# Bucketed attention and a gated product: the first chunk's probabilities in float32, turned by TensorE

## Chip, cores and metric

The kernel runs on one core of one Trainium2 chip. The metric is the device time of one execution in microseconds (us); the number given is the median of three runs. One execution was profiled as well.

The engines are TensorE (PE in the profile; its weight loads are PEld), VectorE (DVE), ScalarE (ACT), GpSimd (POOL) and SyncE (SP). SP issues all DMAs of this kernel, the plain ones and those that turn (transpose) a tile of 16-bit numbers on its way.

## The reference

```python
# q, k, v: (4, 8, 768, 64); proj: (64, 6); w_a, w_b: (512, 1536); w_out: (1536, 512)
q_bits = (np.einsum('bhsd,dk->bhsk', q, proj) > 0); k_bits = (np.einsum('bhsd,dk->bhsk', k, proj) > 0)
q_bucket, k_bucket = sum(bits * 2 ** arange(6))      # 64 buckets
mask = q_bucket[:, :, :, None] == k_bucket[:, :, None, :]
scores = np.where(mask, q @ k.T / sqrt(64), -1e9)
attn = np.exp(scores - max); attn = attn / (sum + 1e-9)
x = (attn @ v), heads side by side                   # (3072, 512)
out = ((x @ w_a) * (x @ w_b)) @ w_out                # (3072, 512) float32
```

Attention is computed only between queries and keys whose six sign bits agree. Its output feeds a gated product of two matrices and a third one.

## The kernel before, in words

Work is cut into 12 chunks: 4 batches of 3 chunks of 256 query rows, with all 8 heads. A chunk has 16 tiles, one for each head and block of 128 query rows (`qtile`), in two halves of 8. A tile is named by batch, chunk, half, pair of heads in the half, head in the pair and block of rows.

Numbers of float32 accuracy are kept as a high and a low float16 part, so that TensorE works on float16 throughout. For each pair of heads K is split (`kprep`): the natural layout is scaled and cut into parts, turned so that the head dimension lies on the partitions, multiplied with `proj` (`buckets`), the six signs are written as extra columns, and a second tile with the signs is turned too. That makes two turned tiles per pair, kTB and kTA. `turn` does a turn in one of two ways: by one transposing DMA (queue SP), or by twelve TensorE transposes into PSUM and a copy of PSUM by ACT or DVE. In batch 0 the first `K_BY_PE` pairs take TensorE, all others DMA. Q goes the same way (`qprep`).

A tile then runs through these steps, with their lines in the profile:
- scores, two times two products of 384 columns (PE, L1029), into a PSUM buffer of two
- the row's maximum (DVE, L1041), its width and bias (L1050, L1057 or L1063)
- the exponential, with the row sums as a by-product (ACT, L1073), into e, float32. Its bias holds ln 2^14, so that the float16 parts keep their accuracy
- a cast of e to float16 (DVE L1081, ACT L1082 or POOL L1083) and the rest e - hi (POOL L1093 or DVE L1097), into the two halves of a2
- one transposing DMA of a2 to at (L1103)
- 18 products of 64 columns, hi x V hi, hi x V lo, lo x V hi (PE, L1112), into the half's av

V is split into vh and vl for this (`vprep`: the maximum by L755 or L758, vh by L793, vl by L805). At a half's end av is divided by the sums (`su_end`), and at a chunk's end x is scaled and turned; for the first and the last chunk by eight float32 transposes on TensorE (px, L1250), for the others by DMA.

The second stage (`moe`) takes a chunk's turned x: 24 groups of 12 products (ab, L1313) with the two first matrices, a gate on ACT and DVE (L1327, L1335), a split of it (L1343, L1355), and 12 groups of 6 products with the third matrix (o, L1365). Before that the 18 blocks of weights are loaded and split as well: an ACT pass (L554), the low words (ACT L562 or POOL L568), a merge on DVE (L577), the high half (ACT L654, POOL L657 or DVE) and the low half (POOL L662 or DVE L666).

Nothing is scheduled while the kernel runs. `Plan` records each step as an operation with an engine, possibly with alternatives on other engines, and the list `ORDER` names operations in the order in which they are issued: a number n below 10000 is operation n, 10000 + n its first alternative, 20000 + n its second. A negative entry -n puts n filler products on TensorE (`fill`, tile "warm", L1469), whose results are not used. Each engine works through its own instructions strictly in this order, and so does SP's queue.

Of the kernel before, what the change touches and what calls it, by code (L numbers as in the profile page):

```python
# [21 lines left out]
P = 128  # L22
# [53 lines left out]
def constants():  # L76
# [17 lines left out]
K_BY_PE = 4  # L94
# [289 lines left out]
def attention_moe(ctx: ExitStack, tc: tile.TileContext, q, k, v, proj, w_a, w_b, w_out, cst, cst_w, out):  # L384
# [341 lines left out]


    HOME_K0 = [("wo0", 1, cp), ("wo1", 1, cp), ("raw", NRAW, p2), ("raw", NRAW, p2)]
    HOME_V0 = [("a2", NA, p2)] * 2 + [("at", NAT, p2)] * 2
    xT, kT, vv, qT, xs, tsq = {}, {}, {}, {}, {}, {}  # L730

    def load_heads(src, b, h0, n, name, key, hold=(), home=("raw", NRAW, p2)):
# [775 lines left out]
```

## Time and profile before

| what | value |
|---|---|
| median of three runs | 901.48 us (900.17 to 902.36) |
| the profiled execution's own time | 899.88 us |
| its span, first to last instruction | 898.1 us |
| PE busy | 858.3 us (96%) |
| DVE busy | 652.5 us (73%) |
| ACT busy | 548.6 us (61%) |
| POOL busy | 450.3 us (50%) |

The span is what the profile covers; some 1.8 us of the execution lie around it. Busy time is summed over the whole span and says nothing about a stage. A matmul's busy time includes the end of its pipeline, so matmuls that follow each other overlap: what one costs TensorE is read from start to start. The filler products count as busy.

### The profile page before, as it was taken

To read this page: it belongs to the slowest core of one execution; us is meant where nothing else is said; L and a number is where in the kernel's file an instruction comes from. 1 tells how busy PE (TensorE), PEld (TensorE's weight loads), DVE (VectorE), ACT (ScalarE), POOL (GpSimd) and SP (SyncE) were. 2 spreads that over 40 slices of the span, in tenths; PEclk is the share of its full clock that TensorE was granted. 3 is DMA by queue.
4 is the path that set the end of the run, shared out by engine and by line. 5 is a ranking of instruction groups with operands and counts; after the bars stand their busy time and mean duration, and the time that the engine had idled before them with its cause. 6 is when DMAs were issued, how large, how long until landed. Compare 5 with 4: busy or idle time off the path is not lost.

```text
span 898.1 us, 23606 instructions
## 1 busy us (share of the span) xinstructions
PE 858.3 (96%) x9444; PEld 652.4 (73%) x9444; DVE 652.5 (73%) x1564; ACT 548.6 (61%) x1056; POOL 450.3 (50%) x389
## 2 busy tenths in 40 slices
PE   4778899999999999999999999999999999999997
PEld 3566677777777777777777777777777777777775
DVE  6999998988887669778876766777888854752210
ACT  6999899987655656556653556645566545543222
POOL 2468957776527653552533263673543545452111
PEclk9999999999999999999999999999999999999999
DMA  8799999999998999978869689898899966754000
GB/s 311 240 270 272 178 237 236 185 205 195 204 183 169 155 170 183 194 153 176 167 125 157 102 159 176 155 206 159 151 194 165 157 116 115 118 102 72 1 25 24
DMA packets 435806, 147.37 MB, mean 164 GB/s; under 512 B 407408, under 2 KB 428016, under 8 KB 435696
## 3 DMA queue, kind: packets, MB, share of 16 engines
q1 hardware_dynamic: 435696, 145.86, 83.4%
q8 instruction: 74, 1.21, 0.6%
q14 instruction: 36, 0.29, 0.1%
HBM read 37.82 MB, written 6.29 MB: 49 GB/s over the span
## 4 chain that ended last, share of the span: by engine, by line
PE 77%; DVE 7%; ACT 3%; DMA 2%; issue 2%; POOL 0%; ACTq 0%; DVEq 0%; POOLq 0%; SPq 0%
PE ab L1313 38%; PE o L1365 19%; PE s L1029 11%; PE av L1112 9%; DMA at<-a 2%; DVE mx L1041 2%; ACT e L1073 1%; DVE xz L1215 1%; ACT a L1082 1%; DVE g L1335 0%; DVE wab L577 0%; PE b_q L819 0%; PE b_k L819 0%; DVE wmx L638 0%; DVE width L1050 0%
## 5 line engine op out<-in xcount | busy, mean ns | idle before, releaser
L1313 PE MATMUL ab<-xT,wab 128*128 128x256 f16 x3456 | 407.7, 273 | 2.2 <-DVE g L1335 2.2
L1313 PEld LDWEIGHTS <-wab 128*128 128x128 f16 x3456 | 332.3, 98 | 55.2 <-issue 2.8
L1093 POOL TENSOR_TENSOR a<-e,a 128x768 f16<-128x768 f32 x147 | 251.2, 1714 | 111.9 <-ACT a L1082 50.2
L1073 ACT ACTIVATE e<-s,bias,width 128x768 f32<-128x768 f32 x192 | 189.7, 988 | 61.1 <-DVE bias L1063 49.1
L1355 POOL TENSOR_TENSOR g<-g,g 128x256 f16<-128x256 f32 x144 | 102.1, 709 | 244.2 <-ACT g L1343 150.8
L1365 PE MATMUL o<-wo,g 128*128 128x512 f16 x864 | 208.7, 379 | 0.0
L1041 DVE TENSOR_REDUCE mx<-s 128x1 f32<-128x768 f32 x192 | 181.5, 949 | 35.2 <-PE s L1029 34.5
L1335 DVE SCALAR_TENSOR_TENSOR g<-ab,wlow,a 128x256 f32<-128x256 f32 x132 | 63.4, 481 | 139.3 <-ACT a L1327 127.0
L1327 ACT ACTIVATE a<-ab,wcut 128x256 f32<-128x256 f32 x144 | 67.7, 470 | 156.7 <-PE ab L1313 148.9
L1112 PEld LDWEIGHTS <-at 128*128 128x128 f16 x3456 | 122.3, 98 | 29.2 <-DMA at<-a 10.9
L1365 PEld LDWEIGHTS <-g 128*128 128x128 f16 x864 | 81.4, 98 | 74.7 <-issue 0.2
L1112 PE MATMUL av<-vh,at 128*128 128x64 f16 x2304 | 126.3, 193 | 9.1 <-DMA at<-a 8.6
L1029 PE MATMUL s<-kTA_k,qTA_q 128*128 128x384 f16 x384 | 93.8, 326 | 5.1 <-ACT e L1073 2.6
L1029 PE MATMUL s<-kTB_k,qTB_q 128*128 128x384 f16 x384 | 93.8, 326 | 0.0
L1082 ACT CAST a<-e 128x768 f16<-128x768 f32 x95 | 78.4, 828 | 2.8 <-DMA at<-a 1.4
L1083 POOL CAST a<-e 128x768 f16<-128x768 f32 x54 | 46.5, 860 | 53.7 <-ACT e L1073 48.2
L1112 PE MATMUL av<-vl,at 128*128 128x64 f16 x1152 | 65.1, 193 | 0.0
L1057 ACT ACTIVATE bias<-mx,width 128x1 f32<-128x1 f32 x98 | 28.4, 292 | 55.9 <-DVE width L1050 55.7
L1343 ACT CAST g<-g 128x256 f16<-128x256 f32 x97 | 38.8, 400 | 35.6 <-DVE g L1335 30.6
L1029 PEld LDWEIGHTS <-qTB_q 128*128 128x128 f16 x384 | 37.5, 98 | 24.9
L1029 PEld LDWEIGHTS <-qTA_q 128*128 128x128 f16 x384 | 34.4, 98 | 24.6 <-issue 8.3
L1097 DVE TENSOR_TENSOR a<-e,a 128x768 f16<-128x768 f32 x45 | 43.5, 967 | 3.8 <-ACT a L1082 3.4
(151 smaller groups left out, 824.3 us busy)
## 6 DMA issues: line engine op xcount, KB each, us to landing
rk_k<-in_k_dram SPq DMA_DIRECT2D x16, 384.0 KB, 4.4
rq_q<-in_q_dram SPq DMA_DIRECT2D x12, 512.0 KB, 5.0
vr<-in_v_dram SPq DMA_DIRECT2D x16, 384.0 KB, 4.2
raw_w<-in_moe_w_b_dram SPq DMA_DIRECT2D x12, 512.0 KB, 5.8
raw_w<-in_moe_w_a_dram SPq DMA_DIRECT2D x12, 512.0 KB, 6.2
raw_wo<-in_moe_w_out_dram SPq DMA_DIRECT2D x12, 512.0 KB, 6.1
out_dram<-ob SPq DMA_DIRECT2D x24, 256.0 KB, 3.1
at<-a SPq DMA_TRANSPOSE x192, 4.2
```

Of the source, the lines that this page charges most:

```text
L1029: nc.tensor.matmul(ps.t[:, jj, :HALF], lhsT=x.t[:, uq, :], rhs=y.t[:, h * NT + jj * 3 : h * NT + jj * 3 + 3, :].rearrange("p t x -> p (t x)"),
L1041: lambda: nc.vector.tensor_reduce(out=mx.t[:, u : u + 1], in_=halves(ps.t), axis=AX.XY, op=ALU.max, negate=True),
L1073: lambda: nc.scalar.activation(flat2(e.t), halves(ps.t), AF.Exp, bias=bias.t[:, u : u + 1], scale=width.t[:, u : u + 1], accum_out=sm.t[:, ...
L1082: ("ACT", 0.725, lambda: nc.scalar.copy(out=a2.t[:, 0], in_=e.t), False),
L1083: ("POOL", 0.9, lambda: nc.gpsimd.tensor_copy(out=a2.t[:, 0], in_=e.t), False),
L1093: lambda: nc.gpsimd.tensor_tensor(out=a2.t[:, 1], in0=e.t, in1=a2.t[:, 0], op=ALU.subtract),
L1112: nc.tensor.matmul(av.t[:, u, :], lhsT=at.t[:, a + kt, :], rhs=w.t[:, h, kt, :], start=i == 0, stop=i == 3 * NT - 1,)
L1313: nc.tensor.matmul(pl.t[:, m, :CH], lhsT=wt(m, wi, cc, f), rhs=xt.t[:, :, xi * NC + cc, :], start=i == 0, stop=i == 3 * NC - 1,)
L1327: lambda a=a, pl=pl, gr=gr: nc.scalar.activation(a.t, pl.t[:, 0, :CH], AF.Copy, scale=wcut[:, gr : gr + 1]),
L1335: lambda a=a, g32=g32, pl=pl, cut=cut: nc.vector.scalar_tensor_tensor(out=g32.t, in0=pl.t[:, 1, :CH], scalar=cut, in1=a.t, op0=ALU.mult, o ...
L1355: lambda g=g, g32=g32: nc.gpsimd.tensor_tensor(out=g[1].t, in0=g32.t, in1=g[0].t, op=ALU.subtract),
L1365: nc.tensor.matmul(po.t[:, u, :], lhsT=g[gi].t[:, us], rhs=wo[f // 2].t[:, f % 2, wi * DM : (wi + 1) * DM], start=f % per_q == 0 and i == ...
```

## The change

Three things are done, and the list `ORDER` is another one.

1. The first chunk of batch 0 (`F32_UNITS = ((0, 0),)`, 16 tiles) no longer splits its probabilities. e stays float32, six TensorE transposes turn it into PSUM (tile et), ACT or DVE copies it to SBUF (tile ec), and six float32 products of 64 columns multiply it with V as it was loaded (v32, tile vr). For these tiles the cast, the subtraction, the transposing DMA and the 18 float16 products are gone; the exponential's bias and the division are adapted, since nothing is scaled there.
2. `K_BY_PE` goes from 4 to 2: the pairs 2 and 3 of batch 0 are turned by DMA, two turns each, like those of all other batches.
3. V's pairs 0 to 3 of batch 0 are loaded into other buffers (`HOME_V0`): three of tag "at" and one of tag "a2".

```diff
-K_BY_PE = 4
+K_BY_PE = 2
+F32_UNITS = ((0, 0),)
...
 ORDER = [
-    1, 5, 7, 2, 4, 13, 0, 41, 53, 61, 8, 300, 301, 27, 10014, 3, 9, 297, 6, 10, 296, 11, 15, 16, 277, 17, 278, 274,
...
-    HOME_V0 = [("a2", NA, p2)] * 2 + [("at", NAT, p2)] * 2
-    xT, kT, vv, qT, xs, tsq = {}, {}, {}, {}, {}, {}
+    HOME_V0 = [("at", NAT, p2)] * 3 + [("a2", NA, p2)]
+    xT, kT, vv, v32, qT, xs, tsq = {}, {}, {}, {}, {}, {}, {}
...
         vr = load_heads(v, b, 2 * hp, 2, f"vr_{n}", key, hold=[vh, vl], home=("raw", NRAW, p2) if b else HOME_V0[hp])
+        v32[b, hp] = vr
...
+    def by_pe(n, b, hp, h, u, e, av, key):
+
+        ps = psum(f"et_{n}", "o")
+
+        def blocks():
+            for kt in range(NT):
+                nc.tensor.transpose(
+                    out=ps.t[:, kt // 3, kt % 3 * P : (kt % 3 + 1) * P], in_=e.t[:, kt * P : (kt + 1) * P], identity=ident
+                )
+
+        op("PE", 0.66, blocks, key, r=[e, "ident"], w=[ps])
+        et = buf("a2", [P, S], F32, f"ec_{n}", NA)
+        op(
+            "ACT", 0.8, lambda: nc.scalar.copy(out=flat2(et.t), in_=halves(ps.t)), key, r=[ps], w=[et],
+            alt=[("DVE", 0.87, lambda: nc.vector.tensor_copy(out=flat2(et.t), in_=halves(ps.t)), False)],
+        )
+        w = v32[b, hp]
+
+        def outs():
+            for kt in range(NT):
+                nc.tensor.matmul(
+                    av.t[:, u, :], lhsT=et.t[:, kt * P : (kt + 1) * P], rhs=w.t[:, h, kt, :],
+                    start=kt == 0, stop=kt == NT - 1,
+                )
+
+        op("PE", 0.72, outs, key, r=[et, w], w=[(av, u)])
+
...
+        whole = (b, c) in F32_UNITS
+        top = 0.0 if whole else LN_ESC
...
+        if whole:
+            by_pe(n, b, hp, h, u, e, av, key)
+            return
         a2 = buf("a2", [P, 2, S], F16, f"a2_{n}", NA)
...
+            if (b, c) in F32_UNITS:
+                nc.scalar.activation(r.t, sm.t, AF.Copy, scale=1.0, bias=1e-9)
+                return
```

The new list has 186 filler products in place of 330. The numbers in it count other operations than before, so the two lists can't be laid side by side; the instructions that they make can.

TensorE, around the scores of the last tile of the first chunk, before. The names end in the tile's place (batch, chunk, half, pair, head, rows) and a buffer number; s is a tile of scores.

```order
L1469 LDWEIGHTS ident16_65
L1469 MATMUL warm_217<-ident16_65 128x256
L1029 LDWEIGHTS qTA_q0_0_389
L1029 MATMUL s_0_0_1_1_1_1_1382<-kTA_k0_3_1117,qTA_q0_0_389 128x384
L1029 LDWEIGHTS qTA_q0_0_389
L1029 MATMUL s_0_0_1_1_1_1_1382<-kTA_k0_3_1117,qTA_q0_0_389 128x384
L1029 LDWEIGHTS qTB_q0_0_297
L1029 MATMUL s_0_0_1_1_1_1_1382<-kTB_k0_3_785,qTB_q0_0_297 128x384
L1029 LDWEIGHTS qTB_q0_0_297
L1029 MATMUL s_0_0_1_1_1_1_1382<-kTB_k0_3_785,qTB_q0_0_297 128x384
L1112 LDWEIGHTS at_0_0_1_0_0_1_1309
L1112 MATMUL av_0_0_1_1340<-vh_0_2_1182,at_0_0_1_0_0_1_1309 128x64
```

TensorE at the same place, of the change:

```order
L1056 MATMUL s_0_0_1_1_1_0_1162<-kTB_k0_3_694,qTB_q0_0_260 128x384
L1023 MATMUL et_0_0_1_1_0_0_1170<-ident_64,e_0_0_1_1_0_0_1150 128x128 x6
L1037 MATMUL av_0_0_1_1122<-vr_0_2_745,ec_0_0_1_0_1_1_1160 128x64 x6
L1056 LDWEIGHTS qTA_q0_0_371
L1056 MATMUL s_0_0_1_1_1_1_1189<-kTA_k0_3_882,qTA_q0_0_371 128x384
L1056 LDWEIGHTS qTA_q0_0_371
L1056 MATMUL s_0_0_1_1_1_1_1189<-kTA_k0_3_882,qTA_q0_0_371 128x384
L1056 LDWEIGHTS qTB_q0_0_260
L1056 MATMUL s_0_0_1_1_1_1_1189<-kTB_k0_3_694,qTB_q0_0_260 128x384
L1056 LDWEIGHTS qTB_q0_0_260
L1056 MATMUL s_0_0_1_1_1_1_1189<-kTB_k0_3_694,qTB_q0_0_260 128x384
L1023 MATMUL et_0_0_1_1_0_1_1198<-ident_64,e_0_0_1_1_0_1_1177 128x128 x6
```

Before, that tile's scores stand between fillers and the 18 products of a tile six places back (0_0_1_0_0_1), which had gone by cast, subtraction and DMA. Now, six transposes and six float32 products of tiles three and four places back stand ahead of them, and no fillers.

ACT, over the last exponentials of the first chunk, before:

```order
L1082 CAST a2_0_0_1_1_0_0_1360<-e_0_0_1_1_0_0_1316 128x768
L1073 ACTIVATE e_0_0_1_1_0_1_1371,sm_0_0_1_1122<-s_0_0_1_1_0_1_1298,bias_0_0_1_1119,width_0_0_1_1078 128x768
L654 CAST wab_78<-wab_78 128x2x512
L1073 ACTIVATE e_0_0_1_1_1_0_1411,sm_0_0_1_1122<-s_0_0_1_1_1_0_1364,bias_0_0_1_1119,width_0_0_1_1078 128x768
L1057 ACTIVATE bias_0_0_1_1119<-mx_0_0_1_1073,width_0_0_1_1078 128x1
L1082 CAST a2_0_0_1_1_0_1_1429<-e_0_0_1_1_0_1_1371 128x768
L1073 ACTIVATE e_0_0_1_1_1_1_1451,sm_0_0_1_1122<-s_0_0_1_1_1_1_1382,bias_0_0_1_1119,width_0_0_1_1078 128x768
L1082 CAST a2_0_0_1_1_1_0_1456<-e_0_0_1_1_1_0_1411 128x768
L1082 CAST a2_0_0_1_1_1_1_1494<-e_0_0_1_1_1_1_1451 128x768
```

ACT at the same place, of the change:

```order
L1102 ACTIVATE e_0_0_1_1_0_0_1150,sm_0_0_1_966<-s_0_0_1_1_0_0_1070,bias_0_0_1_950,width_0_0_1_944 128x768
L1030 COPY ec_0_0_1_0_1_1_1160<-et_0_0_1_0_1_1_1143 128x768
L1102 ACTIVATE e_0_0_1_1_0_1_1177,sm_0_0_1_966<-s_0_0_1_1_0_1_1096,bias_0_0_1_950,width_0_0_1_944 128x768
L1030 COPY ec_0_0_1_1_0_0_1187<-et_0_0_1_1_0_0_1170 128x768
L1086 ACTIVATE bias_0_0_1_950<-mx_0_0_1_909,width_0_0_1_944 128x1
L1102 ACTIVATE e_0_0_1_1_1_0_1205,sm_0_0_1_966<-s_0_0_1_1_1_0_1162,bias_0_0_1_950,width_0_0_1_944 128x768
L1030 COPY ec_0_0_1_1_0_1_1210<-et_0_0_1_1_0_1_1198 128x768
L1102 ACTIVATE e_0_0_1_1_1_1_1230,sm_0_0_1_966<-s_0_0_1_1_1_1_1189,bias_0_0_1_950,width_0_0_1_944 128x768
L1030 COPY ec_0_0_1_1_1_0_1240<-et_0_0_1_1_1_0_1220 128x768
```

Before, casts (a2) of earlier tiles and a high half of the weights (wab) stand between the exponentials. Now a copy of a turned tile (ec<-et) stands behind each exponential, most often that of the tile before it.

SP's queue, before, in the second half of the first chunk:

```order
L1103 DMA_TRANSPOSE at_0_0_1_0_0_0_1205<-a2_0_0_1_0_0_0_1163 128x12x128
L533 DMA raw_w4_1_1165<-in_moe_w_a_dram 128x1024
L847 DMA_TRANSPOSE qTA_q0_1_1292<-marked_79 128x16x128
L1103 DMA_TRANSPOSE at_0_0_1_0_0_1_1309<-a2_0_0_1_0_0_1_1196 128x12x128
L1103 DMA_TRANSPOSE at_0_0_1_0_1_0_1369<-a2_0_0_1_0_1_0_1222 128x12x128
L1103 DMA_TRANSPOSE at_0_0_1_0_1_1_1407<-a2_0_0_1_0_1_1_1279 128x12x128
L1103 DMA_TRANSPOSE at_0_0_1_1_0_0_1427<-a2_0_0_1_1_0_0_1360 128x12x128
L952 DMA rq_q0_2_86<-in_q_dram 128x8x128
L1103 DMA_TRANSPOSE at_0_0_1_1_0_1_1500<-a2_0_0_1_1_0_1_1429 128x12x128
L1103 DMA_TRANSPOSE at_0_0_1_1_1_0_1527<-a2_0_0_1_1_1_0_1456 128x12x128
L1103 DMA_TRANSPOSE at_0_0_1_1_1_1_1559<-a2_0_0_1_1_1_1_1494 128x12x128
```

SP's queue, of the change, in the stretch that holds the turns of K's pairs 2 and 3 (nB_k0_2, nB_k0_3 and twice "marked"):

```order
L847 DMA_TRANSPOSE kTB_k0_2_585<-nB_k0_2_375 128x12x128
L952 DMA rq_q0_1_85<-in_q_dram 128x8x128
L532 DMA raw_w2_1_605<-in_moe_w_a_dram 128x1024 x2
L847 DMA_TRANSPOSE kTB_k0_3_694<-nB_k0_3_594 128x12x128
L847 DMA_TRANSPOSE kTA_k0_2_731<-marked_79 128x12x128
L737 DMA vr_0_2_745<-in_v_dram 128x2x384
L532 DMA raw_w5_0_773<-in_moe_w_b_dram 128x1024
L847 DMA_TRANSPOSE qTB_q0_1_844<-nB_q0_1_727 128x16x128
L847 DMA_TRANSPOSE kTA_k0_3_882<-marked_79 128x12x128
L532 DMA raw_w5_1_907<-in_moe_w_b_dram 128x1024
L737 DMA vr_0_3_942<-in_v_dram 128x2x384
L532 DMA raw_w4_0_979<-in_moe_w_a_dram 128x1024
```

Before, the queue is mostly turned tiles of the first chunk. Now none of these is left; four turns of K stand earlier, among the loads of weights (raw_w), Q (rq) and V (vr).

## Rows read from the trace of the kernel before

**Rows 1.** The page: tenths busy in 40 slices of 22.5 us.
```profile
PE   4778899999999999999999999999999999999997
...
DVE  6999998988887669778876766777888854752210
ACT  6999899987655656556653556645566545543222
```

**Rows 2.** Windows: stretch, its length, each engine's busy time (instructions), granted clock, DMA share, GB/s.
```profile
0.00:11.20 11.20, 0.55 (x2) 0.21 (x2) 3.53 (x12) 3.18 (x6) 1.45 (x9) 1.00 0.68 219
11.20:112.80 101.60, 81.58 (x993) 62.59 (x993) 95.90 (x251) 94.96 (x143) 70.86 (x44) 1.00 1.03 258
...
200.00:800.00 600.00, 598.20 (x6657) 454.48 (x6654) 449.83 (x1058) 341.90 (x710) 293.22 (x263) 1.00 0.88 160
800.00:898.00 98.00, 93.60 (x811) 70.52 (x808) 22.80 (x53) 27.62 (x60) 22.54 (x28) 1.00 0.18 36
```

**Rows 3.** Waits of PE from 11.2 to 112.8 us: total, times, longest.
```profile
PE av L1112 <- DMA at<-a: 6.9, 6, 2.1
...
PE s L1029 <- ACT e L1073: 2.0, 5, 0.5
```

**Rows 4.** PE in time: start, length, line, tile, count, idle time before.
```profile
13.18 2.76 PE L1469 MATMUL warm<-ident 128*128 128x256 f16 x12
...
33.44 0.83 PE L858 MATMUL t_k_DVE<-ident,nB_k 128*128 128x128 f16 x12 [0.74 <-ACT e L1073]
34.11 1.25 PE L1469 MATMUL warm<-ident 128*128 128x256 f16 x10
...
112.85 1.09 PE L1250 MATMUL px<-ident,x 128*128 128x128 f32 x8 [0.26 <-POOL x L1236]
113.78 0.22 PE L594 MATMUL ps_w<-ident,wmx 128*128 128x128 bf16 x1
...
117.79 2.79 PE L1313 MATMUL ab<-xT,wab 128*128 128x256 f16 x24
...
166.87 0.34 PE L1112 MATMUL av<-vh,at 128*128 128x64 f16 x6
...
167.40 0.49 PE L1029 MATMUL s<-kTA_k,qTA_q 128*128 128x384 f16 x2
```

**Rows 5.** The chain of waits in time: start, length, engine, count.
```profile
188.10 2.62 PE ab L1313 x24
```

**Rows 6.** ACT's groups, whole span (exponentials first 200 us): busy, mean ns, idle before.
```profile
L1073 ACT ACTIVATE e<-s,bias,width 128x768 f32<-128x768 f32 x47 | 46.3, 986 | 3.7 <-DVE width L1050 1.2 <-DVE bias L1063 0.9 <-DVE wmx L647 0.6
...
L1082 ACT CAST a<-e 128x768 f16<-128x768 f32 x95 | 78.4, 828 | 2.8 <-DMA at<-a 1.4
...
L562 ACT ACTIVATE raw_w<-raw_w 128x1024 int32<-128x1024 uint8 x10 | 11.5, 1147 | 0.0
...
L1395 ACT ACTIVATE ob<-o,osc 128x512 f32<-128x512 f32 x15 | 10.1, 685 | 7.5 <-PE o L1365 7.0 <-DVE ob L1401 0.4
L654 ACT CAST wab<-wab 128x1024 f16<-128x1024 f32 x9 | 9.3, 1034 | 0.0
...
L866 ACT COPY kTB_k<-t_k_DVE 128x1536 f16<-128x1536 f16 x3 | 4.3, 1426 | 0.1
...
L1262 ACT CAST xT<-px 128x1024 f16<-128x1024 f32 x2 | 2.0, 1012 | 0.4 <-PE px L1250 0.4
```

**Rows 7.** DVE's groups, whole span, the same columns.
```profile
L1097 DVE TENSOR_TENSOR a<-e,a 128x768 f16<-128x768 f32 x45 | 43.5, 967 | 3.8 <-ACT a L1082 3.4
...
L666 DVE TENSOR_TENSOR wab<-wab 128x1024 f16<-128x1024 f32 x2 | 2.4, 1212 | 0.0
...
L868 DVE COPY kTA_k<-t_k_ACT 128x1536 f16<-128x1536 f16 x2 | 1.9, 948 | 0.0
```

**Rows 8.** DMA issues: how many, median us to landing.
```profile
at<-a SPq DMA_TRANSPOSE x192, 4.2
```

**Rows 9.** Line 1250 (px): durations in ns, least, median, most; first, last start.
```profile
L1250 PEld LDWEIGHTS px<-ident,x x16: 137/141/143, 112.8 to 833.2; 128*128 128x128 f32 x16
```

More of the change, by code (lines that the diff above doesn't have):

```diff
@@ L1057, in qtile @@
             lambda: nc.scalar.activation(
-                bias.t[:, col], mx.t[:, col], AF.Copy, scale=width.t[:, col], bias=LN_ESC
+                bias.t[:, col], mx.t[:, col], AF.Copy, scale=width.t[:, col], bias=top
             ),
@@ L1063, in qtile @@
                 lambda: nc.vector.tensor_scalar(
-                    out=bias.t[:, col], in0=mx.t[:, col], scalar1=width.t[:, col], scalar2=LN_ESC,
+                    out=bias.t[:, col], in0=mx.t[:, col], scalar1=width.t[:, col], scalar2=top,
                     op0=ALU.mult, op1=ALU.add,
@@ L1143, in su_end @@
         op(
-            "ACT", 0.56, guarded, key, r=[(sm, u) for u in us] + [("vsc", col), ("vsc", col + 1)], w=[r],
+            "ACT", 0.56, guarded, key, r=[(sm, u) for u in us] + ([] if (b, c) in F32_UNITS else [("vsc", col), ("vsc", col + 1)]),
+            w=[r],
         )
```

391 rows, old and new, of the table ORDER are left out of this document.

## The prediction

> **What bounds the kernel now.** I read the page's slices first. TensorE (PE) is full but for the first five of them and the last; in the first eight VectorE (DVE) and ScalarE (ACT) stand at 9 tenths or close [rows 1]. The windows by stage sharpen this. From 200 to 800 us PE works 598.2 of 600 us: nothing is to be gained there but by taking work from PE. Up to 11.2 us the core waits for its first inputs. Between 11.2 and 112.8 us PE is busy 81.6 of 101.6 us, while DVE is busy 95.9 and ACT 95.0 [rows 2]. The reader should not take those 81.6 us for work: in this stretch lie all 330 filler products ("warm"), whose result nobody reads. A product with as many columns is issued every 2.62/24 = 0.109 us [rows 5], so the fillers hold 36.0 us of PE, and with 20.0 us of idle time 56 us of this stretch are empty. The opening is bound by DVE and ACT together, the rest by PE. The opening ends when the first chunk's x is turned (px, at 112.85) and the first matmul of the second stage starts (ab, at 117.79) [rows 4].
>
> So the span is: the moment of that first ab, plus the PE work left behind it, plus some 8 us of waits later on, which this change has no reason to move. I count what the change does to the first two.
>
> **The PE work.** Sixteen tiles lose their 18 f16 products: from the start of the first to the start of what follows is 0.53 us [rows 4], 8.5 us in all. Each gets six float32 transposes of 128x128. The same operation is there already: eight for px start at 112.85, the next product at 113.78 [rows 4], 0.116 us each, 0.70 us for six, 11.2 us for sixteen tiles. Four turns of K (pairs 2 and 3, two each) leave PE: 0.67 us from the start of one to the start of the next row [rows 4], 2.7 us.
>
> The six float32 products of 128x64 per tile are in no row. From below: an f16 product of this size takes 0.53/18 = 0.029 us, 0.18 us per tile. From above: four times the float32 transpose, 0.465 us, 2.8 us per tile. I take the float32 transpose itself, 0.116 us, the only row in which PE reads float32 from both operands: 0.70 us per tile, 11.2 us in all. The Trainium skill ("FP8 and Floating Point Precision", TensorE Precision Notes) says that a true FP32 product takes four passes through the array. Four passes at the f16 pitch would be 0.117 us, and the sum the same; no row shows it.
>
> PE's real work therefore grows by 11.2 + 11.2 - 8.5 - 2.7 = 11.2 us. Most of this lies ahead of the first ab. Counting entries in the two orders there: 16 tiles turned and multiplied in float32 (+22.4), 18 fewer f16 groups (22 before, 4 now: -9.5), four K turns (-2.7), together +10.2. Behind it only 1.0 us more is left.
>
> **The moment of the first ab.** Both orders have 25 exponentials ahead of it, so the same stage of the work is compared. ACT ahead of it:
> - copies of the turned tile out of PSUM, 0 before, 15 now. Not in the trace; ACT's evictions of float32 from PSUM take 0.685 us for 512 columns and 1.012 us for 1024 [rows 6]; half way, 0.85 us: +12.8. (The bounds are the casts, 0.828, and the exponentials out of PSUM, 0.988 [rows 6], which would move it by -0.3 or +2.1.)
> - casts of e to f16, 19 before, 5 now, 0.828 us: -11.6
> - the weights' low words, 10 before, 4 now, 1.147 us (they go to GpSimd): -6.9
> - the weights' high halves, 6 before, 3 now, 1.034 us (to GpSimd too): -3.1
> - evictions of turned K, 7 before, 5 now (Q's two among them), 1.43 us: -2.9 [rows 6]
>
> Sum -11.7 us. DVE: three subtractions e - hi fewer (-2.9), two K evictions fewer (-1.9), one low half of the weights fewer (-1.2) [rows 7], one copy more, taken as the K eviction's 0.95: -5.0 us. Smaller groups of both signs, none above 2 us, are left out.
>
> GpSimd takes what ACT gives up, but it loses 13 of 21 subtractions ahead of the first ab and stands at 70.9 of 101.6 us [rows 2]: it stays below the other two.
>
> DVE and ACT are both about 94% busy there and hand each other work, so the moment should come earlier by something between 5.0 and 11.7 us. I take the middle, 8.4 us.
>
> **What hides the rest.** The two K pairs now make two DMA trips each, at some 4.2 us from issue to landing [rows 8]. On SP the first of pair 2 goes out ahead of the load of Q's chunk 1, the second right after pair 3's first; between pair 2's last trip and its first scores stand, on ACT alone, four exponentials, two of the new copies, two low words and a high half, 4 x 0.986 + 2 x 0.85 + 2 x 1.147 + 1.034 = 9.0 us [rows 6]. Without that cover a trip would cost its 4.2 us once per pair. Behind those transposes SP holds weight loads and V's pairs 2 and 3, used later still. In return SP and the DMA engines lose 16 turns of the same size in this chunk. V in float32 is kept in buffers of the turned tiles, three of which chunk 1 needs; pair 0's is free long before chunk 1's first turn stands in SP's order. I cost both at nothing.
>
> **The sum.** -8.4 + 1.0 = -7.4 us. A second account must agree: PE's real work +11.2, fillers 330 to 186, 144 x 0.109 = -15.7, so idle time has to fall by 2.9 us. It can: six waits for turned tiles, 6.9 us in the opening, all belong to this chunk [rows 3] and vanish; I let 4 us of them come back as waits for ACT's copies. The profiled execution took 899.88 us, so 892.5; it lay 1.6 us under the median of the runs, so the median comes to 894.1 us.
>
> **Rivals.**
> 1. ACT alone sets the opening: -11.7 + 1.0 = -10.7, 890.8 us. For it: five of the list's large items are ACT's. Against it: DVE stands at the same share.
> 2. The new path binds ACT and PE to each other. Before, ACT cast and went on, and only PE waited for the landed tile. Now a copy on ACT waits for PE's transposes, PE waits in order for that copy before the next tile's transposes (the PSUM tag "o" has one buffer), and exponentials and scores queue behind both. PE's waits for exponentials were 2.0 us in five, 0.4 us each [rows 3]; if every tile costs ACT such a wait, 16 x 0.4 = 6.4 us return: 900.5 us, no change. What speaks against it is that in the new order scores of other tiles stand between a tile's transposes and its products.
> 3. Slower: the float32 product costs far more. At four times the transpose PE gets 16 x 2.1 = 33 us more, all in the opening. The fillers are issued whatever happens, so only the idle time takes it up, about 17 us, half of which is real waiting: -7.4 + 33.4 - 8.5 = +17.5, 919 us. It begins to be slower where the extra is 8.5 + 7.4 = 16 us, that is at 1.7 us per tile (0.28 us per product, 2.4 times what I took). The Trainium skill ("TensorE: Matmul & The Clock Gate", Weight-path perf modes) says that fast weight loading is off for FP32. The trace agrees in direction: px's weight loads take 0.141 us at the median [rows 9]. Four loads of that for each product would be 0.56 us, beyond this rival's price; whether a product loads its weights four times no row shows.
> 4. The clock. Twelve fillers at 13.18 us take 2.76 us, 0.23 each, against 0.109 later [rows 4, 5]: the array then ran at 1.2 and not 2.4 GHz, though the granted clock of the stretch is written as 1.00 [rows 2]. PE had done little before. With 144 fillers fewer it could fall back; the real work ahead of ab, some 54 us now, would double, and beyond what idle time takes up the span would grow by about 30 us. Against it: PE has more real work in the stretch than before. The Trainium skill (same page, PE-mode transpose) states that transposes in that mode don't count as PE-busy for the clock; by that rule this rival would gain weight, but scores and fillers remain between them, and no run here shows it.
>
> **Chances and numbers.** Forecast 0.56; ACT alone 0.13; rival 2 0.15; rival 3 0.10; clock 0.03; other ways of being slower, such as a late K pair, 0.03. A measurement of this kernel can tell 0.2%, 1.8 us, from no change. Forecast and rival 1 are faster (0.69), as is a part of rival 2 (0.04): 0.73. The rest of rival 2 is no change (0.11). Slower: 0.16. The forecast's own range runs from ACT's to DVE's bound, 890.8 to 897.5 us. The range given reaches below by the uncertainty of the other waits and above over rival 2 to a mild form of rival 3: 887.5 to 903.5.
>
> **What would show it.** Right: first ab at about 109 us; transposes of six in about 0.7 us and products of six in about 0.7 us; fewer than 40 us of idle time in total; waits for turned tiles gone from the opening; PE full behind it as before. Wrong: six products in 1.7 us or more; PE or ACT waiting for each other tile by tile, with DVE below 90% in the opening; ab's start unmoved; or new gaps on PE after 150 us, where a new order might starve it.

## The result, and the profile after

The changed kernel took 907.44 us (median of five runs, 906.09 to 909.64), the kernel before 901.52 us beside it: a ratio of 1.007, with a 95% interval of 1.0059 to 1.0082. It is slower by 0.7%. The prediction said 894.1 us, 887.5 to 903.5, and gave "slower" 0.16.

The profiled execution has a span of 905.4 us. First the page's slices of 22.6 us, to be laid beside [rows 1]:

```profile
PE   4799899999999998999999999999999999999998
...
DVE  6999999988778787779767667767888865652210
ACT  6897899967655665465653466545666655452212
```

ACT has come off two of its six nines in the opening, and PE has lost a nine far behind it (the sixteenth slice, 340 to 362 us), which nothing in the change asked for. The windows (columns as in [rows 2]; the last line is of before) say how much:

```profile
11.20:112.80 101.60, 87.44 (x833) 72.37 (x834) 94.78 (x232) 86.89 (x134) 66.19 (x45) 1.00 0.77 221
48.00:60.00 12.00, 10.96 (x108) 8.79 (x108) 11.79 (x29) 12.00 (x19) 7.66 (x6) 1.00 0.78 201
60.00:98.00 38.00, 35.85 (x308) 31.36 (x306) 34.24 (x82) 30.45 (x54) 29.72 (x19) 1.00 0.63 171
...
112.97:905.40 792.43, 776.41 (x8415) 588.09 (x8413) 560.80 (x1304) 448.02 (x903) 368.91 (x331) 1.00 0.81 148
200.00:800.00 600.00, 589.80 (x6518) 446.80 (x6516) 450.64 (x1042) 338.85 (x697) 280.85 (x254) 1.00 0.88 158
340.00:370.00 30.00, 25.96 (x260) 18.76 (x258) 20.94 (x55) 15.99 (x35) 12.95 (x12) 0.94 1.01 181
...
117.79:898.10 780.31, 771.87 (x8384) 586.30 (x8380) 548.16 (x1294) 445.43 (x903) 374.79 (x334) 1.00 0.82 151
```

Two things are to be read. The opening now has two parts: from 48 to 60 us ACT is busy 12.00 of 12 (11.61 in before); from 60 to 98 us PE is the fullest, with 35.85 of 38 (30.59 in before). And behind the first ab, where before took 898.1 - 117.8 = 780.3 us, after takes 792.4, 12.1 us more: PE is idle for 16.0 us of it, against 8.4. From 200 to 800 us PE idles 10.2 us, where it idled 1.8 [rows 2].

PE in time, the opening (start, length, line, tile, count, idle before), beside [rows 4]:

```profile
62.33 0.82 PE L1023 MATMUL et<-ident,e 128*128 128x128 f32 x6
62.99 1.15 PE L1505 MATMUL warm<-ident 128*128 128x256 f16 x9
...
78.02 0.82 PE L1023 MATMUL et<-ident,e 128*128 128x128 f32 x6
78.68 2.79 PE L1037 MATMUL av<-vr,ec 128*128 128x64 f32 x24
81.31 0.82 PE L1023 MATMUL et<-ident,e 128*128 128x128 f32 x6
...
105.68 1.09 PE L1286 MATMUL px<-ident,x 128*128 128x128 f32 x8
...
112.97 1.26 PE L1349 MATMUL ab<-xT,wab 128*128 128x256 f16 x10
```

Six transposes take 62.99 - 62.33 = 0.66 us from start to start. The products of two tiles take 81.31 - 78.68 = 2.63 us, so six cost 1.31 us, and each of the twelve products shows as two records. The first ab is at 112.97 us: 4.8 us earlier than before, not 8.4.

Behind it the waits of PE from 113 to 900 us (total, times, longest; the last line is of before, from 117.8 us), and around the two longest of them the timeline of SP's queue, ACT, DVE and PE (put in order of time, from one view per engine):

```profile
PE ab L1349 <- DVE g L1371: 7.3, 7, 2.6
PE av L1144 <- DMA at<-a: 2.4, 4, 1.2
PE s L1056 <- DMA kTA_k<-marked: 1.2, 1, 1.2
...
PE ab L1313 <- DVE g L1335: 2.2, 3, 1.1
```

```profile
340.23 0.57 SPq L737 DMA_DIRECT2D rk_k<-in_k_dram  x1
...
344.77 0.84 ACT L754 ACTIVATE nB_k<-rk_k 128x768 bf16<-128x768 f32 x1 [3.11 <-DMA rk_k<-in_k_dram]
...
346.97 0.48 DVE L1371 SCALAR_TENSOR_TENSOR g<-ab,wlow,a 128x256 f32<-128x256 f32 x1 [2.56 <-ACT a L1363]
...
347.51 1.47 PE L1349 MATMUL ab<-xT,wab 128*128 128x256 f16 x12 [1.36 <-DVE g L1371]
...
358.07 0.57 SPq L737 DMA_DIRECT2D rk_k<-in_k_dram  x1
...
361.82 0.95 DVE L757 TENSOR_REDUCE mx_k<-rk_k 128x1 f32<-128x768 f32 x1 [3.45 <-DMA rk_k<-in_k_dram]
362.69 0.47 DVE L1371 SCALAR_TENSOR_TENSOR g<-ab,wlow,a 128x256 f32<-128x256 f32 x1
...
363.22 4.45 PE L1349 MATMUL ab<-xT,wab 128*128 128x256 f16 x24 [2.55 <-DVE g L1371]
```

The page's name for the wait is "g", but g is not the cause. A load of a tile of K goes out at 340.23 us. ACT's next instruction in its order sums the magnitudes of that very tile and stands idle for 3.11 us until the load has landed; a of the gate is queued behind it on ACT, g waits for a, and ab waits for the PSUM buffer that g empties. At 358.07 us the same happens with the next tile, and it is DVE that waits 3.45 us, with g itself behind. After that stop the 24 products of ab take 4.29 us from their start to that of the next row (367.51 us) instead of 2.62 [rows 5], 1.7 us more (the expectations below count 1.8); the granted clock from 360 to 370 us is 0.83. Over the stretch behind the first ab the single waits of ACT and DVE for loads of K, Q or V come to 19 us (eight waits, from 0.4 to 4.7 us); in the trace of before they come to 5.5 us (five, the longest 2.3).

### The profile page after: what moved, and what is told of

Its sections match the earlier page's. It is cut to its first block, busy times and chain, and to the rows that moved or that the text cites. A ratio compares the mean times of both kernels' runs of the same rounds, so it can differ in the third digit from the quotient of the medians.

```text
span 905.4 us, 23135 instructions
## 1 busy us (share of the span) xinstructions
PE 865.2 (96%) x9252; PEld 661.0 (73%) x9252; DVE 660.1 (73%) x1557; ACT 539.9 (60%) x1043; POOL 437.5 (48%) x384
## 4 chain that ended last, share of the span: by engine, by line
PE 70%; DVE 15%; DMA 6%; ACT 3%; issue 3%; SPq 2%; POOL 1%; ACTq 0%; DVEq 0%; POOLq 0%
PE ab L1349 34%; PE o L1401 16%; PE s L1056 10%; PE av L1144 7%; DMA at<-a 3%; DVE mx L1070 3%; PE av L1037 2%; DMA rq_q<-in_q_dram 1%; ACT e L1102 1%; DVE g L1371 1%; DVE wmx L637 1%; DVE nB_q L907 1%; DMA rk_k<-in_k_dram 1%; DVE wab L576 1%; DVE width L1079 1%
## 5 line engine op out<-in xcount | busy, mean ns | idle before, releaser
L1125 POOL TENSOR_TENSOR a<-e,a 128x768 f16<-128x768 f32 x129 | 217.9, 1691 | 124.4 <-ACT a L1114 59.2
L1363 ACT ACTIVATE a<-ab,wcut 128x256 f32<-128x256 f32 x144 | 67.6, 469 | 110.3 <-PE ab L1349 108.4
L1144 PEld LDWEIGHTS <-at 128*128 128x128 f16 x3168 | 112.1, 98 | 22.3 <-DMA at<-a 4.6
L1144 PE MATMUL av<-vh,at 128*128 128x64 f16 x2112 | 115.4, 193 | 2.4 <-DMA at<-a 2.4
L1115 POOL CAST a<-e 128x768 f16<-128x768 f32 x52 | 44.5, 857 | 62.8 <-ACT e L1102 42.6
L1114 ACT CAST a<-e 128x768 f16<-128x768 f32 x83 | 68.6, 830 | 2.5 <-DMA at<-a 1.0
L1379 ACT CAST g<-g 128x256 f16<-128x256 f32 x103 | 41.4, 402 | 45.6 <-DVE g L1371 38.0
L1086 ACT ACTIVATE bias<-mx,width 128x1 f32<-128x1 f32 x91 | 26.4, 292 | 69.8 <-DVE width L1079 69.4
L1144 PE MATMUL av<-vl,at 128*128 128x64 f16 x1056 | 59.6, 193 | 0.0
L1129 DVE TENSOR_TENSOR a<-e,a 128x768 f16<-128x768 f32 x47 | 47.0, 1002 | 8.4 <-ACT a L1114 6.6
```

The lines of the kernel that those rows point to most:

```text
L1114: ("ACT", 0.725, lambda: nc.scalar.copy(out=a2.t[:, 0], in_=e.t), False),
L1125: lambda: nc.gpsimd.tensor_tensor(out=a2.t[:, 1], in0=e.t, in1=a2.t[:, 0], op=ALU.subtract),
L1129: lambda: nc.vector.tensor_tensor(out=a2.t[:, 1], in0=e.t, in1=a2.t[:, 0], op=ALU.subtract), True,
L1144: nc.tensor.matmul(av.t[:, u, :], lhsT=at.t[:, a + kt, :], rhs=w.t[:, h, kt, :], start=i == 0, stop=i == 3 * NT - 1,)
L1363: lambda a=a, pl=pl, gr=gr: nc.scalar.activation(a.t, pl.t[:, 0, :CH], AF.Copy, scale=wcut[:, gr : gr + 1]),
```

## The experiments

Two theories. **T1**: the products in float32 are too dear, and hold up the opening. **T2**: the new order behind the opening starves PE. Rivals to T2: the later stalls follow from the opening itself; or the engines are simply full there. Rivals to T1: ACT and DVE set the opening alone; the clock. "Before" beside the runs had a median of 900.9 to 901.1 us.

### 1 and 2. The two orders, crossed

```diff
 e1: places 0 to 619 of ORDER as in after (to about 135 us)
-    all later places as in after
+    the remaining operations in the sequence of before
 e2: places 0 to 650 of ORDER as in before
-    all later places as in before
+    the remaining operations in the sequence of after
```

> The changed kernel up to some 135 us (its new opening with the float32 products, the key tiles turned by DMA and its fillers), and behind that the order of the kernel before, operation for operation. Theory A, the new order behind the opening starves TensorE (the trace of after has 16.0 us of idle PE behind its first ab, that of before 8.4, and a stretch of ab at a clock of 0.83 that cost 1.8 us more): both go away, and the time is about 907.4 - 9 = 898 us (896 to 901), with no stall on g above 1 us between 340 and 370 us. Rival B, the later stalls come from the opening itself (another state of buffers and queues behind it, whatever the order): they stay, 906 to 908 us. Rival C, half and half: 902 to 904 us. The opening stays as it is in after, first ab at 113 us, whatever theory holds.

> The mirror of the run before: the kernel before up to its sixth ab or so, and behind that the order of the changed kernel. First ab at 117.8 us as in before. Theory A (the new order behind the opening starves TensorE by itself): 901.5 + 9 = 910 us (907 to 912), with the stalls on g at about 350 to 370 us and a dip of the granted clock there. Rival B (the later stalls are a consequence of the new opening): 901 to 903 us.

The first took 898.81 us (ratio to before 0.9973, 0.996 to 0.9986), the second 910.09 us (1.0095, 1.0075 to 1.0114). From the first ab to the end of the span the profiled executions have 782.1 us with the old order behind (897.1 - 115.0) and 791.1 with the new one (908.6 - 117.5), whichever opening stands ahead. The wait for g of 2.76 us came with the new order, and between 340 and 370 us only one of 0.26 us is left with the old one (run 2, then run 1):

```profile
370.64 2.78 PE L1309 MATMUL ab<-xT,wab 128*128 128x256 f16 x24 [2.76 <-DVE g L1331]
...
342.88 2.78 PE L1345 MATMUL ab<-xT,wab 128*128 128x256 f16 x24 [0.26 <-DVE g L1367]
```

The dip of the granted clock that I expected there in run 2 did not come: it is 1.00 from 360 to 380 us. T2 holds: the order behind costs some 9 us by itself (8.6 and 9.0 by medians), with either opening. The first run is also faster than before, by 0.3%, at full precision. Its first ab came 2 us later than in after, though both run the same program up to there; run 7 and run 11 come back to that.

### 3. The products made cheap

```diff
-    av.t[:, u, :], lhsT=et.t[:, kt * P : (kt + 1) * P], rhs=w.t[:, h, kt, :],
+    av.t[:, u, :], lhsT=upper(et.t[:, kt * P : (kt + 1) * P]), rhs=upper(w.t[:, h, kt, :]),
```

> The changed kernel with the 16 groups of six float32 products read from the upper 16 bits of both operands (bfloat16: the lower 16 bits of the probabilities and of V are left out of these products); everything else, the order too, stays. Theory D, the price of the float32 products (1.31 us for six by the trace of after, 0.70 in the prediction) holds up the opening: six cost about a third of the 0.53 us of a group of eighteen float16 products, some 0.2 us, so PE is relieved of 16 x 1.1 = 18 us between 46 and 98 us, where it is busy 9.6 to 9.8 of 10; DVE, busy 8.5 to 9.2 of 10 there, is next, and the first ab comes 3 to 5 us earlier, at 108 to 110 us, the time 902 to 905 us. Rival E, ScalarE and VectorE with their waits for each other set the opening and PE is full only because its fillers and products fit into their gaps: first ab moves by less than 1 us, 906 to 908 us.

It took 896.1 us (0.9951, 0.9933 to 0.9969). PE in time:

```profile
60.16 0.34 PE L1037 MATMUL av<-vr,ec 128*128 128x64 bf16 x6
60.33 0.49 PE L1056 MATMUL s<-kTA_k,qTA_q 128*128 128x384 f16 x2
...
109.15 1.25 PE L1349 MATMUL ab<-xT,wab 128*128 128x256 f16 x10
```

Six products now take 0.17 us, and the first ab is at 109.15 us, 3.8 us earlier than in after: T1's forecast for the opening. How the dear products had held it up shows on ACT, whose copies wait for transposes that stand behind those products on PE. In after, from 11.2 to 113 us:

```profile
ACT ec L1030 <- PE et L1023: 4.9, 7, 1.4
```

Here 1.0 us of that is left, in two waits. By medians the total fell by 11.3 us, more than was expected of either theory. The span of the profiled execution, at 898.84 us the slowest of its five, fell by 8.7 us: 3.8 ahead of the first ab and 4.9 behind it (896.7 - 109.2 = 787.5 us), where the order is that of after. There some of the stalls are shorter (341 us: 0.73 for 1.36; none at 498 us). This suggests that part of what a bad order costs depends on how the loads happen to fall against it.

### 4. The keys by DMA alone, in the old order

```diff
-K_BY_PE = 4
+K_BY_PE = 2
 ORDER: for pairs 2 and 3 the DMA turn at the place of PE's turn; PSUM copies gone
```

> The kernel before with one part of the change alone: the key tiles of pairs 2 and 3 are turned by DMA, each issued at the place of the PE turn that it replaces, without the copies from PSUM; order, fillers and float16 probabilities as before. If DMA turns are in time, PE is relieved of four turns of 0.7 us (2.7 us) and ScalarE and VectorE of two copies each, the opening gets 0 to 2.5 us shorter: 899 to 901.5 us. Rival, the DMA (4.2 us from issue to landing for a turn of probabilities) comes later than the turn by PE with its copy, and scores wait for the keys: 902 to 905 us, with a wait of s for kTA or kTB.

It took 912.12 us (1.0131, 1.0102 to 1.016), far outside both expectations: the first ab came at 128.1 us. The wait was not the one I had named. ACT in time:

```profile
33.71 0.83 ACT L1078 CAST a<-e 128x768 f16<-128x768 f32 x1
41.49 0.84 ACT L751 ACTIVATE nB_k<-rk_k 128x768 bf16<-128x768 f32 x1 [6.95 <-DMA kTB_k<-nB_k]
```

The turn of pair 2 is issued on SP at 34.24 us and holds the natural tile nB until 41.4 us. There are two such tiles; ACT's next instruction wants to write pair 3 into one of them and stands for 6.95 us, with the exponentials behind it. In before PE's turn had read the tile by 34.1 us [rows 4], and the same instruction ran at 35.64 us. No scores waited for a turned K. The held tile accounts for 41.49 - 35.64 = 5.9 us of the 10.3 by which the first ab came later; behind it the granted clock is 0.65 from 40 to 50 us, where before has 1.00, and how the rest divides is open.

### 5. The two readers of late loads moved

```diff
 ORDER of after:
-    1587: ScalarE, sum of magnitudes of the first tile of K of the third batch (15 places behind its load)
+    moved 12 places, behind a, an exponential and one pass of xz
-    1660: VectorE, maximum of the second tile of K (20 places behind its load)
+    moved 8 places, behind g and three other instructions of VectorE
```

> The changed kernel with two instructions moved in its order and nothing else: the first readers of two K loads of the third batch (the ScalarE instruction that sums the magnitudes of one tile of K, the VectorE one that takes the maximum of the next) stand 12 and 8 places later, so that ScalarE has done a and VectorE g of the expert layer before they wait for their loads. Theory A2, the new order lets an engine that stands in the path of g wait for a load issued only 15 and 20 places ahead (26 and 34 in before), and this is what stops PE at 347.5 and 363.2 us (1.36 and 2.55 us, and 1.8 us more by the clock that fell behind the second): these stalls go, the clock stays at 1.00 there, and the time is 907.4 - 5.7 = 901.7 us (900.5 to 903). Rival, DVE and ACT are simply full there and PE waits whatever they do first: the stalls move by a few us, 905.5 to 908 us.

It took 901.64 us (1.0008, 0.9993 to 1.0022): 5.8 us less than after, where 5.7 were expected. The stretch in the windows view:

```profile
340.00:370.00 30.00, 30.00 (x349) 23.11 (x347) 25.59 (x64) 17.39 (x38) 14.48 (x14) 1.00 1.10 210
```

PE is busy 30.00 of 30 us where after had 25.96, at a clock of 1.00 where it had 0.94. The theory holds and the rival is out. Two instructions out of some 3650 operations account for more than half of what the order behind costs (run 1 gave 8.6). (The profiled execution of this run, 898.64 us, was the fastest of its ten; its 783.3 us behind the first ab flatter it.)

### 6. Both suspects away

```diff
 run 1, and
-    lhsT=et.t[...], rhs=w.t[...]
+    lhsT=upper(et.t[...]), rhs=upper(w.t[...])
```

> The new opening with the products of the upper 16 bits (the lower 16 bits of probabilities and V left out of these 16 groups), and the old order behind 135 us: both suspects taken away at once. If the two costs are independent (products in the opening, order behind it), the time is that of the new opening with the old order, 898.8, less the 3.8 us by which the first ab came earlier with the cheap products: 895.0 us (893.5 to 896.5). If the gain of the cheap products came mostly from another timing of the stalls behind the opening (the run with cheap products and the new order behind was 11.3 us faster, of which 3.8 lay ahead of the first ab), it is more like 898 us. If the granted clock in the opening falls as PE is less busy, up to 3 us come on top.

It took 891.67 us (0.9894, 0.9877 to 0.9912), 7.1 us less than run 1 and beyond my 893.5: the first ab came at 108.4 us against 115.0, and the clock stayed at 1.00 in the whole opening. ACT's waits for transposes before its copies are 0.3 us here and 8.2 in run 1. The price of the products is worth 4 to 7 us on a sound order, the more where their opening loses clock.

### 7. Fewer fillers

```diff
 run 1, ORDER:
-    -16 ... -11 ... -15 ... -9 ... -5
```

> The new opening with the old order behind, without the 56 filler products that stand between the fifth and the eighth float32 tile (about 62 to 85 us, 0.109 us each, 6.1 us), where TensorE is already busy 9.6 to 9.8 of 10. If TensorE is the bound there, the first ab comes 2 to 5 us earlier and the time is 894 to 897 us. If VectorE and ScalarE are the bound there, 898 to 899.5 us. If the clock is held up only by the fillers in this stretch (float32 transposes and products may not hold it), the granted clock falls below 0.9 between 60 and 100 us for 10 us and more and the time is 900 to 905 us.

It took 899.94 us (1.0011, 0.998 to 1.0041), with the first ab at 117.6 us. The expectation had the place wrong: most of these fillers run from 48 to 66 us. In the windows:

```profile
48.00:60.00 12.00, 6.58 (x67) 5.11 (x67) 11.79 (x28) 12.00 (x18) 7.62 (x7) 1.00 0.76 199
76.00:84.00 8.00, 7.20 (x36) 5.66 (x35) 5.74 (x23) 3.27 (x5) 7.51 (x6) 0.57 1.14 334
```

Up to 60 us ACT is busy 12.00 of 12 with or without the fillers: PE is not the bound there, and nothing is gained. From 76 to 84 us the granted clock is 0.57 (0.69 in run 1, 1.00 in after). The median hides two groups: six of the ten executions took 897.7 to 900.4 us with a mean granted clock of 0.992 to 0.996, four took 905.1 to 907.0 us with 0.989. So the third account of the expectation holds for some executions: without the fillers more time is spent at the lower clock. Why the opening was already 1.9 us later than in run 1 at 65 us, at full clock, stays open.

### 8. The disputed price by itself

```diff
-    one pass over the 64 columns of V for each tile
+    parts = [(0, D)] if h else [(0, D // 2), (D // 2, D)]   # every other tile: two passes of 32
```

> The changed kernel with the float32 products of every other tile cut into two passes of 32 columns of V each (24 records of 32 columns in place of 12 of 64; the same result). It measures the disputed price itself. If a record costs its weights (128x128 float32 loaded for each record: 0.1095 us), a cut tile takes 24 x 0.1095 = 2.63 us against 1.31 of a whole one. If a record costs its columns, a cut tile takes 1.31 us like a whole one. The time of the kernel itself rises by up to 8 x 1.31 = 10.5 us in the first case and stays in the second.

One execution, 921.82 us. PE in time, and one window:

```profile
62.30 1.45 PE L1039 MATMUL av<-vr,ec 128*128 128x64 f32 x12
63.59 0.49 PE L1058 MATMUL s<-kTA_k,qTA_q 128*128 128x384 f16 x2
...
66.53 2.76 PE L1039 MATMUL av<-vr,ec 128*128 128x32 f32 x24
69.12 0.71 PE L1507 MATMUL warm<-ident 128*128 128x256 f16 x5
```

```profile
84.00:104.00 20.00, 20.00 (x107) 18.19 (x105) 7.44 (x14) 7.42 (x13) 5.69 (x4) 0.59 0.20 46
```

A whole tile takes 63.59 - 62.30 = 1.29 us, a cut one 69.12 - 66.53 = 2.59: 0.108 us a record with 64 columns and with 32. The price goes with the records and not with the columns: 2 x 6 x 0.108 = 1.30 us. Each record loads 128x128 weights; that this load is the price is likely, but a fixed cost of a float32 record for another reason would look the same here. The window shows something else: PE busy 20.00 of 20 us, and a granted clock of 0.59.

### 9. All late readers moved

```diff
 ORDER of after: run 5, and six more first readers of K and Q, 6 to 14 places later
```

> The changed kernel with eight first readers of loads moved 6 to 14 places later (the two of the run with two moved readers, and six more: of tiles of K and Q in the second to fourth batch, for four of which ScalarE or VectorE waited 1 to 5 us in the traces of after or of that run). Theory A2 (readers placed too near their loads hold up a and g, and by them PE): besides the stalls at 347 and 363 us, those at about 546 and 563 us (0.87 and 0.76 us, behind a wait of 2.9 us of VectorE for a load of Q) go, and the sum of ACT's and DVE's waits for loads falls from 19 us to below 8; the time is 901.6 - 1.6 = 900.0 us (898.5 to 901.5). Rival: these stalls come back elsewhere, since PE has little slack anywhere, 901.5 to 903 us.

It took 901.37 us (1.0006, 0.9991 to 1.002): the same as run 5. ACT's and DVE's waits for loads are all but gone (0.9 us in three are left, of 19). Of the two stalls the first shrank from 0.87 to 0.24 us, and the second is still there at its full 0.76 us, though no engine waits for a load there any more:

```profile
547.61 2.78 PE L1345 MATMUL ab<-xT,wab 128*128 128x256 f16 x24 [0.24 <-DVE g L1367]
...
564.78 1.47 PE L1345 MATMUL ab<-xT,wab 128*128 128x256 f16 x12 [0.76 <-DVE g L1367]
```

PE still waits 2.5 us for turned tiles and 2.3 us for g behind the first ab, as much for g as in before (2.2). The rival holds here: what is left of T2 is spread over many places of the order and is not the readers.

### 10. The float32 path alone, in the old order

```diff
 after, and
-K_BY_PE = 2
+K_BY_PE = 4
 ORDER of before: transpose at the cast's place, copy behind it, products at the old products' place; fillers 330 to 175
```

> The other part of the change alone: the kernel before with float32 probabilities in the first chunk, in the old order: each transpose stands where the cast to float16 stood, its copy a few places behind, the six float32 products where the eighteen float16 products stood (six of them up to 16 places earlier, so that the buffers suffice, and one eviction of K and one normalisation earlier for the same reason); all four pairs of key tiles turned by PE as before, fillers cut from 330 to 175. PE gets 10.5 us of transposes and 21.0 us of products for 8.5 us of the old ones, less 16.9 us of fillers: +6 us of work. If the opening is not bound by PE in this order, the release of DVE and of the DMA turns shows: 897 to 901 us. If the products at 1.31 us stand in the way of scores in PE's in-order queue, as they stand thick in the opening: first ab later than 117.8 us by 2 to 6 us, 903 to 908 us. The second is taken as likelier.

It took 935.96 us (1.0383, 1.0359 to 1.0408), with the first ab at 151.5 us: the likelier side of the expectation, but more than five times its upper end. In the windows:

```profile
90.00:130.00 40.00, 31.75 (x173) 25.31 (x172) 18.00 (x44) 18.18 (x30) 5.74 (x3) 0.63 0.12 27
```

DVE and ACT are busy less than half of this stretch, and the clock is 0.63. By the waits PE stands 9.8 us before transposes for their exponentials, and while it stands, the scores that the next exponentials need stand behind the transposes in its queue. ACT stands longer, 18.9 us in five waits between 91 and 123 us, before copies that need a buffer which a float32 product has yet to read. The first of them:

```profile
98.30 0.80 ACT L1027 COPY ec<-et 128x768 f32<-128x768 f32 x1 [6.45 <-PE av L1034]
```

The products stand late in PE's order, where the old ones stood; the copies wait for them, the exponentials stand behind the copies on ACT, and PE waits for the exponentials. So this is the price of that placement and of the clock, and not of the float32 path in any order.

### 11. Fillers in three gaps

```diff
 run 1, ORDER: behind the last scores ahead of the gaps, the signs of Q, and one maximum of V
+    -2, -4, -4
```

> The new opening with the old order behind, and ten filler products more (1.1 us), put into the three gaps between 71 and 75 us where PE waits for ScalarE and VectorE (0.24, 0.47 and 0.52 us). In the profiled execution of the run without them the granted clock fell to 0.5 between 73 and 81 us, right at these gaps, and the first ab came at 115.0 us; in the executions of the same opening profiled in after and in the run with two moved readers it stayed at 1.00 and the first ab came at 113.0 and 113.2. If the gaps let the clock fall, fillers in them hold it up in every execution: 898.8 - 2 = 896.8 us (895.5 to 898), with less spread among the executions. If it falls for another reason (the float32 transposes and products around them), 898.5 to 900 us and the same spread.

It took 897.96 us (0.9964, 0.995 to 0.9978), between the two expectations. Windows from 72 to 84 us, of run 1 and of this run:

```profile
72.00:84.00 12.00, 10.91 (x76) 9.26 (x75) 9.45 (x29) 7.04 (x13) 11.48 (x10) 0.72 0.96 292
```

```profile
72.00:84.00 12.00, 11.80 (x112) 10.42 (x112) 11.21 (x30) 9.40 (x16) 11.57 (x9) 1.00 0.93 291
```

In the profiled execution the clock stayed up and the first ab came at 112.3 us, 2.7 us earlier than in run 1. Three other profiled executions of this opening (after, runs 5 and 9) kept their clock without these fillers, and the medians differ by 0.9 us, within their uncertainty. The other executions say more. In run 1 seven of ten have a mean granted clock of 0.996 and took 898.7 to 899.5 us, and three have 1.000 and took 895.8 to 897.5: the dip costs some 2.4 us. With the ten fillers all ten executions have 0.999 or 1.000. So the expectation that fillers hold the clock in every execution is borne out (the two runs were on different chips). That the idle gaps are what lets it fall is not shown: in run 6 PE is idle for 4.0 of these 12 us, against 1.1 in run 1, and has 1.00.

## Why the prediction was wrong, point by point

**The opening's bound** was read rightly for the kernel before. ACT's busy time ahead of the first ab fell by 103.1 - 91.9 = 11.3 us (11.7 were counted), DVE's by 104.4 - 99.3 = 5.0 us (5.0 counted); the copies, taken at 0.85 us, measured 0.79.

**The float32 product** is the term that was mis-sized: 0.70 us per tile taken, 1.31 measured (run 8 says why: two records per product, 0.108 us each, with 32 columns as with 64). PE's real work rose by 10.5 + 21.0 - 8.5 - 2.7 = 20.3 us (with transposes at 0.66 and products at 1.31), not by 11.2. The value came from "the only row in which PE reads float32 from both operands", a transpose; that row has one record per block and the product has two, so that the price per record was nearly right and the number of records wrong. The Trainium skill's four passes ("FP8 and Floating Point Precision", TensorE Precision Notes) gave 0.117 us a product by the f16 pitch; measured are 0.219, so here the measurement decides. The Trainium skill's other rule, fast weight loading off for FP32 ("TensorE: Matmul & The Clock Gate", Weight-path perf modes), agrees in direction with run 8, in which the price goes with the records, each with a load of its own.

**The moment of the first ab**: 8.4 us earlier forecast, 4.8 measured. With the same order and cheap products it is 117.8 - 109.2 = 8.6 us (run 3), and 9.4 at a clock of 1.00 throughout (run 6). The middle between DVE's and ACT's release was thus near for a PE that is not in the way. It is not a test of the forecast itself: those products cost 0.17 us per tile, and no run shows what 0.70 would have given. The dear products put PE in the way from 60 to 98 us.

**"Some 8 us of waits later on, which this change has no reason to move"** is the step that failed most. The change came with an order searched anew, 3679 entries of which the diff is mostly made, and I compared the two only ahead of the first ab. Behind it, it lost 12.1 us: 7.6 of idle time on PE and 4.5 of busy time, of which 1.0 was predicted and about 1.7 is ab at the lower clock after the stall at 363 us; the other 1.8 I have not traced. Crossing the orders gave and took this (runs 1 and 2); two readers placed 15 and 20 places behind their loads, 26 and 34 in before, are more than half of what crossing gives (run 5). The rest, 2.8 us by medians (901.6 against 898.8), is not pinned to any single place (run 9). In the profiled executions the account closes: the opening gave 3.6 us less than forecast and the stretch behind it took 11.1 us more than the 1.0, together the 14.7 us between a span 7.4 us shorter and one 7.3 us longer.

**The second account** asked idle time to fall by 2.9 us. It rose, from 39.8 to 40.2 us: what the opening gave was lost behind it.

**K by DMA "at nothing"** held in the new order, where no score of the first batch waited for a key. But the cover ahead of the scores, which I gave as the reason, is not enough: in the old order no score waited for a key either, and the edit cost 11 us, beginning with a held buffer (run 4). The float32 path, put at the places of the old steps, cost 35 (run 10). Neither part gains anything in the old opening as it was placed there, so the new order of the opening belongs to the change.

**The rivals.** The third, slower by dearer products, had the right mechanism; at 1.31 us it is below the 1.7 at which I let it decide, and alone it would still have left the kernel faster, as run 1 shows. The clock had a chance of 0.03; it cost about 1.7 us behind a stall in after and some 2 us in the opening of run 1. ACT and PE binding each other was priced at 6.4 us: in after ACT stands 4.9 us before copies for their transposes (seven waits), and PE 2.5 us for copies, where I had let 4 come back. ACT's share came by way of the dear products, since with cheap ones 1.0 us of it is left (run 3). Run 10 shows how far this can go. The sign that decided it, "new gaps on PE after 150 us, where a new order might starve it", stood in the list of what would prove me wrong, without a price.

## What to carry to other kernels

A change that brings a new order is two changes: compare the orders to the end, above all how far behind each load its first reader stands, and who is queued behind that reader on its engine. The name on a wait is that of the last link; follow it back over the in-order engines until something waits for a transfer. Where no row has an operation, ask into how many records it will be cut: an operand's type alone did not give the price. And ask who fills a buffer next: a tile that a transfer holds for 7 us, where TensorE held it for 0.7, moves the wait there.

## What the hardware showed unexpectedly

- A float32 product of 128x128 by 128x64 is two records of 0.108 us, and one of 32 columns costs the same; a float32 transpose of 128x128 is one record of 0.11 us.
- TensorE can be busy all the time and still be granted the lower clock for most of it: 20.00 of 20 us at 0.59 in run 8, in a stretch of float32 products, transposes and scores. The Trainium skill says of transposes alone that they don't count as PE-busy in the same way for the clock ("TensorE: Matmul & The Clock Gate", PE-mode transpose); products were most of that stretch, so the rule cannot be told apart from other causes here.
- The same program up to 135 us ran with a granted clock of 1.00 from 72 to 84 us in one profiled execution and of 0.72 in another (runs 5 and 1), and its first ab came at 113.2 and at 115.0 us. Run 1 by itself has both: a mean granted clock of 0.996 in seven executions and of 1.000 in three, some 2.4 us apart. Ten filler products held it in all ten executions of run 11; what decides it without them is open.
